# Writing both parts of the first layer's weights to DRAM in the first batch and loading them ready-made in batches 2 to 4

## The chip, the cores and the metric

The kernel runs on one core of a Trainium2 chip. The metric is the device time of one launch in microseconds (us). Five engines have instruction streams of their own: TensorE (PE, matmuls), VectorE (DVE), ScalarE (ACT), GpSimd (POOL) and SyncE (SP, which here issues every DMA). They meet only at semaphores, and each takes its own instructions strictly in order, so an instruction that waits holds up everything behind it on its engine.

## The reference

```
attention:  phi(x) = [exp(p), exp(-p)],  p = x w_phi - max|x w_phi|       (q, k: 4 x 8 x 576 x 64, 128 features)
            out = phi(q) (phi(k)^T v) / (phi(q) sum phi(k) + 1e-6)        -> x: 2304 x 512
layer 1:    h = x w_in (512 x 2048);  g = max(0.01 h, h);  x = g w_out (2048 x 512)
layer 2:    4 experts: x = sum_e p_e * (relu(x w1_e) w2_e)                (512 x 1024, 1024 x 512)
```

All inputs and the output are float32 except w_in and w_out, which arrive as 64-bit floats.

## The kernel before

**Two parts.** Most float32 operands are split into a high part, rounded to the matmul's `fp32r` format, and a low part, the rest. `hilo` (L113) makes them: one copy (ACT for the weights, L117) and one subtraction on DVE (L118). A product is then three matmuls: high by high, high by low, low by high.

**Stages.** The four batches' attention, layer 1 and layer 2 overlap. `attn` (L415) gives each attention step a due time from a table, `moe1_group` (L550) makes the steps of layer 1, and all steps are sorted by due time and recorded (L860). A scheduler then fixes the order on each engine. Layer 1 of batch b is interleaved with the attention of batch b + 1, so the x of a batch (tiles `xh`, `xl`, made by `x_mul`, L367) is due when its layer 1 begins. The last step of the attention chain runs: the denominators `ds` by DMA (L352), a reciprocal on DVE (L359, L360), a store `dr` (L362), a broadcast load `rb` (L364), two multiplications `xr` (L378), then `xh` on ACT and `xl` on DVE. Layer 2 begins at about 640 us.

**Layer 1.** A batch has 16 blocks of 128 hidden columns, F = 0 to 15 in the first batch. `moe1_up` (L494) multiplies x by one w_in tile into the PSUM tile `hp` (24 matmuls of 288 columns, L503), ACT scales it (`hs`, L515), DVE takes the maximum (`g`, L517), and `hilo` makes `gt`. `moe1_down` (L526) multiplies four blocks' `gt` with four w_out tiles into `op` (L535, 24 matmuls for each of four output slices); DVE adds to `acc` (L548). `ORDER` (L26) mixes the four up blocks of a group with the four down slices of the group before. `hp`, `op` and `pq` share three PSUM buffers (`ps2`, L101).

**The weights of layer 1.** Names in the traces: `r` from w_in or w_out is the 64-bit raw tile (two blocks, 1024 KB), `w` the float32 tile (128x512, pool `wrp`), `wt` the tile with both parts (128x1024, pool `wp`), `w_0_f` or `w<-w` the DRAM copy, `wr` a float32 tile loaded back.

- In the first batch, `w64_split` (L449) turns a block of 64-bit numbers into float32 with one ACT instruction (L457) and three on DVE (L458, L461, L464), sends the float32 tile to DRAM (L468) and splits it into `wt`.
- In batches 2 to 4, `w_dma` (L430) loads the float32 tile back into a `wr` tile and `w_split` (L434) splits it again, with one ACT copy and one DVE subtraction for each of 2 x 16 x 3 = 96 tiles.
- `w` and `wr` tiles share the four buffers of `wrp`. A `w` buffer is free when the split has read it and its store to DRAM has landed. `wt` tiles have seven buffers; the first layer-2 weights also use them (L664, L671).

Of the kernel before, what the change touches and what calls it, by code (L numbers as in the profile page):

```python
# [7 lines left out]
F32 = mybir.dt.float32  # L8
F32R = mybir.dt.float32r
# [5 lines left out]
B, H, S, D = 4, 8, 576, 64  # L15
# [51 lines left out]
VHI = ({"g", "w"}, {"k", "q"}, {"k"})  # L67

N_U = 19
N_W = 7  # L70
N_G = 6
N_X = 10

# [6 lines left out]
def body(ctx, tc, kT, qT, vh, w_phi, w_in, w_out, probs, w1, w2, out):  # L80
    nc = tc.nc
# [5 lines left out]
    drw = ec(tc.tile_pool(name="drw", bufs=1, space=bass.MemoryType.DRAM))  # L87

    def opened(stack, name, bufs, **kw):
        return stack.enter_context(  # L90
            tc.tile_pool(name=name, bufs=bufs, reuse_waits="tile", **kw)
        )


    left, left0, right = ExitStack(), ExitStack(), ExitStack()
    up = opened(right, "up", N_U, side="right")
    wp = opened(left0, "wp", N_W)
    vp = opened(left0, "vp", 2)
    wrp = opened(left0, "wrp", 4)
    gp = opened(left0, "gp", N_G)  # L100
    ps2 = opened(left0, "ps2", 3, space=bass.MemoryType.PSUM)  # L101
    ps1 = opened(left0, "ps1", 2, space=bass.MemoryType.PSUM)
# [10 lines left out]
    def hilo(hi, lo, src, name, b):  # L113
        if name in VHI[min(b, 2)]:
            nc.vector.tensor_copy(hi, src)
        else:
            nc.scalar.copy(out=hi, in_=src)  # L117
        nc.vector.tensor_tensor(out=lo, in0=src, in1=hi.bitcast(F32), op=ALU.subtract)  # L118
# [296 lines left out]
    def attn(b, lo, hi):  # L415

        A = []
        for p in range(NP):
            T = TIMES[p if b == 0 else NP]
            for t, (f, h, a) in zip(T, STEPS):  # L420
                i = p if h is None else 2 * p + h
                A.append((p + t, lambda f=f, i=i, a=a: f(b, i, *a)))
        A.sort(key=lambda x: x[0])
        t0, t1 = A[0][0], A[-1][0]
        return [(lo + (hi - lo) * (t - t0) / (t1 - t0), f) for t, f in A]


    raw = {}

    def w_dma(key, src):  # L430
        raw[key] = wrp.tile([128, 512], F32, tag="wr", name="wr")
        nc.sync.dma_start(out=raw[key], in_=src)

    def w_split(key, b, r=None):  # L434
        t = wp.tile([128, 2, 512], F32R, tag="w", name="wt")
        hilo(t[:, 0], t[:, 1], raw.pop(key) if r is None else r, 'w', b)
        return t

    def w64_dma(i, f):

        t = xp.tile([128, 2, 512, 2], U32, tag="x", name="r64")
        nc.sync.dma_start(
            out=t.rearrange("p a c t -> p a (c t)"),
            in_=(w_in, w_out)[i][f : f + 2].bitcast(U32).rearrange("a p c -> p a c"),
        )
        raw[i, f] = t[:, 0]
        raw[i, f + 1] = t[:, 1]

    def w64_split(i, f):  # L449

        r = raw.pop((i, f))
        lo, hi = r[:, :, 0], r[:, :, 1]
        w = wrp.tile([128, 512], F32, tag="wr", name="w32")
        wu = w.bitcast(U32)


        nc.scalar.activation(out=w, in_=hi.bitcast(F32), func=AF.Abs, scale=2.0**-112)  # L457
        nc.vector.tensor_scalar(  # L458
            out=wu, in0=wu, scalar1=3, scalar2=None, op0=ALU.logical_shift_left
        )  # L460
        nc.vector.scalar_tensor_tensor(  # L461
            out=wu, in0=hi, scalar=0x80000000, in1=wu, op0=ALU.bitwise_and, op1=ALU.bitwise_or
        )
        nc.vector.scalar_tensor_tensor(  # L464
            out=wu, in0=lo, scalar=29, in1=wu, op0=ALU.logical_shift_right, op1=ALU.bitwise_or
        )
        d = drw.tile([128, 512], F32, name=f"w32_{i}_{f}")
        nc.sync.dma_start(out=d, in_=w)  # L468
        w32[i, f] = d
        return w_split(None, 1, w)  # L470

    w32 = {}
    wt1 = {}

    def w1_dma(i, F):
        b, f = divmod(F, NF)
        if b == 0:
            if f % 2 == 0:
                w64_dma(i, f)
        elif b < B:  # L480
            w_dma((i, F), w32[i, f])

    def w1_split(i, F):
        b, f = divmod(F, NF)
        if b < B:
            wt1[i, F] = w64_split(i, f) if b == 0 else w_split((i, F), b + 1)

    PASS = ((0, 0), (0, 1), (1, 0))
    accs = {}
# [60 lines left out]
    def moe1_group(G):  # L550


        def up(F, n):
            if n == 0:
                w1_dma(0, F + 2)
                w1_split(0, F + 1)
                w1_dma(1, F)
            elif F:
                w1_split(1, F - 1)
            moe1_up(F, n)  # L560

        def down(d, n):
            if G == B * NF // GF and d == 0 and n == 0:
                w1_split(1, G * GF - 1)
            moe1_down(G - 1, d, n)

        M = []
        for kind, i in ORDER:
            if kind == "u" and G < B * NF // GF:
                M += [lambda i=i, n=n: up(G * GF + i, n) for n in range(2)]  # L570
            elif kind == "d" and G > 0:
                M += [lambda i=i, n=n: down(i, n) for n in range(2)]
        return M
# [88 lines left out]
    def w2_dma(c):  # L662

        pool, tag = (m2["r"], "r") if m2 else (wp, "w")  # L664
        r = pool.tile([128, 4, 256], F32, tag=tag, name="r")
        nc.sync.dma_start(out=r[:, 2:4].rearrange("p a f -> p (a f)"), in_=w1[2 * c])
        nc.sync.dma_start(out=r[:, 0:2].rearrange("p a f -> p (a f)"), in_=w1[2 * c + 1])
        return r
# [170 lines left out]
    def spread(fs, lo, hi):  # L839
        return [(lo + (hi - lo) * i / len(fs), f) for i, f in enumerate(fs)]  # L840

    def first():
        w1_dma(0, 0)
        w1_dma(1, 0)
# [5 lines left out]
    for b in range(B):  # L850
# [3 lines left out]
        if b + 1 < B:  # L854
            a = attn(b + 1, b + LO[b], b + HI[b])
        else:
            early = x2_steps(0)
            a = spread(early[:4], b + 0.1, b + 0.9)
# [10 lines left out]
    r = w2_dma(0)  # L869
# [17 lines left out]
    r = w2_dma(1)  # L887
    r2 = w2_dma_d(0)
    nxt = []
    for k in range(n):  # L890
        j, c = divmod(k, NC2)
# [4 lines left out]
        r = w2_dma((k + 2) % NC2) if k + 2 < n else None  # L896
# [38 lines left out]
```

## Time and profile before

| | |
|---|---|
| median of 3 runs | 1399.87 us (1398.96 to 1400.92) |
| the profiled execution | 1398.86 us, span 1397.1 us |
| PE busy | 1355.4 us (97%) |
| DVE, ACT, POOL busy | 816.9, 658.4, 572.7 us |
| granted TensorE clock, mean | 0.989 |

The span runs from the first instruction to the last; the execution's own time is 1.8 us longer. Overlapping matmuls count as busy PE, so PE time is lost where PE waits for another engine, or where its granted clock is low. PE stalls, their releasers and the chain that ended last are what to read; a busy share of another engine says little by itself.

### The profile page before, as it was taken

What the parts mean: (1) busy time and instruction counts of PE and PEld (TensorE: products, weight loads), DVE (VectorE), ACT (ScalarE), POOL (GpSimd) and SP (SyncE); (2) the same over time, 40 slices, a digit from 0 to 9 for tenths busy, and PEclk for the clock granted to TensorE, in tenths of its full rate; (3) what the DMA queues carried; (4) which work ended last, traced back from release to release, by engine and by line L of the source; (5) the groups of instructions that cost most, each with busy time, mean ns of one, the idle gap of its engine ahead of it and who ended that gap; (6) DMA issues with size and microseconds to landing.
All of it is one profiled execution on the core that took longest, in us unless ns stands there. A gap on an engine that the chain in (4) does not pass through costs nothing.

```text
span 1397.1 us, 21274 instructions
## 1 busy us (share of the span) xinstructions
PE 1355.4 (97%) x8105; PEld 1264.4 (91%) x8105; DVE 816.9 (58%) x1285; ACT 658.4 (47%) x1201; POOL 572.7 (41%) x398
## 2 busy tenths in 40 slices
PE   8769989999999999999999999999999999999998
PEld 6668989999999999998999899999999999999997
DVE  5359879877777566554454544454445544454445
ACT  5547755676566544433344433444344333333331
POOL 3123101111111000015676675667677675656551
PEclk9979999999999999999999999999999999999999
DMA  6348554333332232222211221321212131212111
GB/s 218 95 120 299 199 201 126 124 107 102 113 102 78 78 105 79 69 69 76 76 61 61 76 69 67 112 70 61 76 62 74 61 119 63 76 61 76 61 61 61
DMA packets 78038, 134.94 MB, mean 97 GB/s; under 512 B 11760, under 2 KB 22128, under 8 KB 77936
## 3 DMA queue, kind: packets, MB, share of 16 engines
q1 hardware_dynamic: 77936, 133.58, 29.2%
q8 instruction: 64, 1.05, 0.3%
q14 instruction: 38, 0.31, 0.1%
HBM read 120.30 MB, written 13.18 MB: 96 GB/s over the span
## 4 chain that ended last, share of the span: by engine, by line
PE 86%; DMA 6%; DVE 4%; issue 2%; ACT 1%; POOL 0%; SPq 0%; DVEq 0%; ACTq 0%; POOLq 0%
PE po L758 28%; PE op L535 13%; PE hp L503 12%; PE py L719 11%; PE pv L719 7%; PE px L719 7%; PE kvp L242 4%; PE nm L335 2%; DMA rb<-dr 2%; DMA qraw<-qT 2%; PE pk L204 2%; DMA w<-w 1%; DMA r<-w_in 1%; PE pq L292 1%; DVE w L461 1%
## 5 line engine op out<-in xcount | busy, mean ns | idle before, releaser
L758 PE MATMUL po<-wd,gh 128*128 128x512 f32 x1152 | 387.4, 391 | 0.9 <-POOL wd L711 0.9
L774 DVE SCALAR_TENSOR_TENSOR ob<-po,pe,ob 128x512 f32<-128x512 f32 x270 | 201.6, 749 | 216.5 <-PE po L758 216.5
L758 PEld LDWEIGHTS po<-wd,gh 128*128 128x128 f32 x1152 | 216.3, 188 | 42.5 <-POOL wd L711 1.3
L535 PE MATMUL op<-gt,wt 128*128 128x288 f32 x1536 | 222.7, 299 | 6.7 <-DVE g L517 5.3
L296 POOL PARTITION_ALL_REDUCE mb<-pc x32 | 76.9, 2406 | 370.8 <-ACT pc L294 312.6
L758 PE MATMUL po<-wd,gl 128*128 128x512 f32 x576 | 226.0, 392 | 0.0
L503 PE MATMUL hp<-xh,wt 128*128 128x288 f32 x1024 | 216.1, 298 | 3.3 <-ACT xh L117 3.3
L535 PEld LDWEIGHTS op<-gt,wt 128*128 128x128 f32 x1536 | 210.3, 190 | 8.4 <-DVE g L517 5.8
L503 PEld LDWEIGHTS hp<-xh,wt 128*128 128x128 f32 x1024 | 167.5, 188 | 4.3 <-ACT xh L117 3.6
L503 PE MATMUL hp<-xl,wt 128*128 128x288 f32 x512 | 152.2, 297 | 0.4 <-DVE xl L118 0.4
L711 POOL TENSOR_TENSOR wd<-r,wd 128x1024 fp32r<-128x1024 f32 x48 | 115.1, 2397 | 88.8 <-ACT wd L707 88.8
L719 PE MATMUL py<-xo,wuh 128*128 128x384 f32 x576 | 148.2, 338 | 0.7 <-DVE pz L824 0.7
L679 POOL TENSOR_TENSOR rs<-r 128x256 f32<-128x256 f32 x96 | 71.3, 744 | 188.1 <-DMA r<-w 188.1
L701 POOL TENSOR_TENSOR wul<-rs,wuh 128x1024 fp32r<-128x1024 f32 x48 | 115.5, 2406 | 66.2 <-ACT wuh L696 66.2
L701 POOL TENSOR_TENSOR wul<-r,wuh 128x768 fp32r<-128x768 f32 x48 | 88.9, 1851 | 84.9 <-ACT wuh L696 84.9
L758 PEld LDWEIGHTS po<-wd,gl 128*128 128x128 f32 x576 | 108.1, 188 | 15.3
L719 PEld LDWEIGHTS py<-xo,wuh 128*128 128x128 f32 x576 | 104.9, 188 | 4.6 <-DVE pz L824 1.0
L719 PE MATMUL pv<-xo,wuh 128*128 128x384 f32 x384 | 99.0, 339 | 0.0
L719 PE MATMUL px<-xo,wuh 128*128 128x384 f32 x384 | 98.6, 338 | 0.0
L503 PEld LDWEIGHTS hp<-xl,wt 128*128 128x128 f32 x512 | 96.4, 188 | 1.1 <-DVE xl L118 0.7
L719 PE MATMUL py<-xo,wul 128*128 128x384 f32 x288 | 97.2, 338 | 0.0
L804 ACT COPY py<-px 128x384 f32<-128x384 f32 x48 | 22.2, 463 | 143.6 <-PE px L719 137.5
(114 smaller groups left out, 2349.7 us busy)
## 6 DMA issues: line engine op xcount, KB each, us to landing
r<-w SPq DMA_DIRECT2D x192, 256.0 KB, 2.6
wr<-w SPq DMA_DIRECT2D x96, 256.0 KB, 3.3
qraw<-qT SPq DMA_DIRECT2D x32, 288.0 KB, 7.1
r<-w_out SPq DMA_DIRECT2D x9, 1024.0 KB, 9.0
r<-w_in SPq DMA_DIRECT2D x8, 1024.0 KB
w<-w SPq DMA_DIRECT2D x32, 256.0 KB, 2.2
v<-vh SPq DMA_DIRECT2D x16, 480.0 KB, 3.9
kraw<-kT SPq DMA_DIRECT2D x16, 288.0 KB, 5.1
```

The source lines that it names most:

```text
L204: nc.tensor.matmul(o, lhsT=x[:, cs], rhs=w, start=(i == 0), stop=(i == len(P) - 1))
L242: nc.tensor.matmul(kvp[:, a * 128 : (a + 1) * 128], lhsT=lhs, rhs=v[:, c, h * D : h * D + 128], start=(c == 0), stop=(c == 4),)
L296: nc.gpsimd.partition_all_reduce(mb, pc, 128, bass_isa.ReduceOp.absmax)
L335: nc.tensor.matmul(o, lhsT=a[:, 2 * (h % 2) + j], rhs=x[:, j * HS : (j + 1) * HS], start=(j == 0 and i == 0), stop=(j == 1 and i == len(P) ...
L503: nc.tensor.matmul(hp[:, n, 0:HS], lhsT=wi[:, a, kk * 128 : (kk + 1) * 128], rhs=x[z][:, kk, n * HS : (n + 1) * HS], start=(kk == 0 and i ...
L535: nc.tensor.matmul(op[:, n, 0:HS], lhsT=wt1[1, C * GF + f][:, a, d * 128 : (d + 1) * 128], rhs=gts[C * GF + f][:, z, n * HS : (n + 1) * HS ...
L679: kept(nc.gpsimd.tensor_tensor(out=o, in0=x, in1=y, op=op))
L701: kept(nc.gpsimd.tensor_tensor(out=lo[:, at], in0=(r[:, 1:4], s)[i], in1=hi[:, at].bitcast(F32), op=ALU.subtract))
L711: kept(nc.gpsimd.tensor_tensor(out=d[:, 1], in0=r2, in1=d[:, 0].bitcast(F32), op=ALU.subtract))
L719: kept(nc.tensor.matmul(out, lhsT=ws[w][:, AOPS[a], kk * 128 : (kk + 1) * 128], rhs=xo[z][:, kk], start=first and n == 0, stop=n == 5, ski ...
L758: kept(nc.tensor.matmul(op, lhsT=(gh, gl)[z][:, 2 * f + t, q : q + 128], rhs=d[:, w, f], start=n == 0, stop=n == 5,))
L774: kept(nc.vector.scalar_tensor_tensor(out=o, in0=op, scalar=ps, in1=o, op0=ALU.mult, op1=ALU.add))
```

## The change

In the first batch the store to DRAM now takes the finished `wt` tile with both parts (128x1024, 512 KB) in place of the float32 tile (256 KB), so it is issued after the split. In batches 2 to 4 each tile is loaded from there straight into a `wt` buffer, and the 96 copies and 96 subtractions are gone. `w_dma`, `w_split` and the `wr` tiles are gone too; the load is issued in `w1_split`, and waits for a free `wt` buffer. `wp` has eight buffers for seven, `wrp` two for four.

```diff
-N_W = 7
+N_W = 8
...
-    wrp = opened(left0, "wrp", 4)
+    wrp = opened(left0, "wrp", 2)
...
-    def w_dma(key, src):
-        raw[key] = wrp.tile([128, 512], F32, tag="wr", name="wr")
-        nc.sync.dma_start(out=raw[key], in_=src)
-
-    def w_split(key, b, r=None):
-        t = wp.tile([128, 2, 512], F32R, tag="w", name="wt")
-        hilo(t[:, 0], t[:, 1], raw.pop(key) if r is None else r, 'w', b)
-        return t
...
-        d = drw.tile([128, 512], F32, name=f"w32_{i}_{f}")
-        nc.sync.dma_start(out=d, in_=w)
+        t = wp.tile([128, 2, 512], F32R, tag="w", name="wt")
+        hilo(t[:, 0], t[:, 1], w, 'w', 1)
+        d = drw.tile([128, 1024], F32, name=f"w32_{i}_{f}")
+        nc.sync.dma_start(out=d, in_=t.bitcast(F32).rearrange("p a c -> p (a c)"))
         w32[i, f] = d
-        return w_split(None, 1, w)
+        return t
...
     def w1_dma(i, F):
         b, f = divmod(F, NF)
-        if b == 0:
-            if f % 2 == 0:
-                w64_dma(i, f)
-        elif b < B:
-            w_dma((i, F), w32[i, f])
+        if b == 0 and f % 2 == 0:
+            w64_dma(i, f)
 
     def w1_split(i, F):
         b, f = divmod(F, NF)
-        if b < B:
-            wt1[i, F] = w64_split(i, f) if b == 0 else w_split((i, F), b + 1)
+        if b == 0:
+            wt1[i, F] = w64_split(i, f)
+        elif b < B:
+            t = wp.tile([128, 2, 512], F32R, tag="w", name="wt")
+            nc.sync.dma_start(
+                out=t.bitcast(F32).rearrange("p a c -> p (a c)"), in_=w32[i, f]
+            )
+            wt1[i, F] = t
```

The scheduler makes a new order from this. Lines after the change are numbered lower: L448 is the old L457, L449, L452 and L455 are L458, L461 and L464, L511 and L513 are L515 and L517, L433 is L442; L461 is now the store of a `wt` tile and L479 the load of one.

**Place 1: ACT, late in the first batch, around the conversion of block 15 of w_in (`w32_2199` before, `w32_2197` after).** `hs_1900` belongs to block 11. In brackets stand the semaphores that an instruction waits for; those that begin with DMAHW count landed DMAs. Before:

```order
L275 CAST qr_1875<-qraw_1832 128x576 [waits DMAHW1_49]
L342 COPY nf_1824<-nm_1865 128x288 [waits PE_49]
L342 COPY nf_1747<-nm_1869 128x288 [waits PE_49]
L457 ACTIVATE w32_2199<-r64_1907 128x512 [waits DMAHW4_49,DVE_49]
L515 ACTIVATE hs_1900<-hp_1852 128x576 [waits PE_49]
L117 CAST wt_2045<-w32_2038 128x512
```

After:

```order
L342 COPY nf_1824<-nm_1865 128x288 [waits PE_49]
L342 COPY nf_1747<-nm_1869 128x288 [waits PE_49]
L511 ACTIVATE hs_1900<-hp_1852 128x576 [waits PE_49]
L117 CAST wt_2043<-w32_2038 128x512 [waits DMAHW4_49,DVE_49]
L117 CAST gt_1904<-g_1902 128x576 [waits DVE_49]
L117 CAST wt_2066<-w32_2061 128x512 [waits DMAHW0_49,DVE_49]
L511 ACTIVATE hs_1956<-hp_1921 128x576 [waits PE_49]
L448 ACTIVATE w32_2197<-r64_1907 128x512 [waits DVE_49]
```

The conversion has moved behind `hs_1900` and waits for no DMA any more; the copies into `wt` now wait for one, the store of the tile that had the buffer before.

**Place 2: SP, from the last store of `dr` in the first batch to the load of `rb` that follows it.** Before:

```order
L362 DMA dr<-ds 128x9
L432 DMA wr<-w_0_1_622 128x512
L468 DMA w_1_13_2238<-w_2233 128x512
L166 DMA qraw<-qT 128x576
L442 DMA r_2209<-w_out 128x2x1024
L364 DMA rb<-dr 128x1x576
```

After:

```order
L362 DMA dr<-ds 128x9
L166 DMA qraw<-qT 128x576
L433 DMA r_2207<-w_out 128x2x1024
L461 DMA w_0_15_2205<-wt 128x1024
L364 DMA rb<-dr 128x1x576
```

Before, a load into `wr` and the store of block 13 of w_out's float32 tile stood ahead of `qraw`, the 1024 KB load and `rb`; now `qraw` and the large load go first, and `rb` stands behind the store of block 15 of w_in, which waits for that block's subtraction.

**Place 3: DVE, the conversions of four tiles late in the first batch: 1909 and 2038 (w_in, blocks 13 and 14), 1934 and 2061 (w_out, blocks 11 and 12).** After:

```order
L118 TENSOR_TENSOR wt<-w_1909,wt 128x512
L118 TENSOR_TENSOR wt<-w_1934,wt 128x512
L118 TENSOR_TENSOR gt<-g,gt 128x576
L449 TENSOR_SCALAR w_2038<-w_2038 128x512
L276 TENSOR_TENSOR qr<-qraw,qr 64x576
L452 SCALAR_TENSOR_TENSOR w_2038<-r_1907,w_2038 128x512
L449 TENSOR_SCALAR w_2061<-w_2061 128x512
```

Tile 2038 has the buffer of 1909, and 2061 that of 1934: two and four DVE instructions stand between the subtraction that frees a buffer and the first DVE instruction on the next tile, and in that time ACT must have run L448. Before, with four buffers, the same two tiles' first instructions stood ahead of the subtraction of 1934:

```order
L118 TENSOR_TENSOR wt<-w_1909,wt 128x512
L458 TENSOR_SCALAR w_1934<-w_1934 128x512
L458 TENSOR_SCALAR w_2038<-w_2038 128x512
L461 SCALAR_TENSOR_TENSOR w_1934<-r_1780,w_1934 128x512
L461 SCALAR_TENSOR_TENSOR w_2038<-r_1907,w_2038 128x512
L458 TENSOR_SCALAR w_2061<-w_2061 128x512
```

What has moved is how far the conversions run ahead of each other.

## Rows read from the trace of the kernel before

**Rows 1.** The page: busy us, share of the span, instructions of each engine.

```profile
PE 1355.4 (97%) x8105; PEld 1264.4 (91%) x8105; DVE 816.9 (58%) x1285; ACT 658.4 (47%) x1201; POOL 572.7 (41%) x398
```

**Rows 2.** Busy time by window: length, PE, PEld, DVE, ACT, POOL, clock, DMA share, GB/s.

```profile
250.00:625.00 375.00, 374.82 (x2882) 374.78 (x2883) 258.19 (x392) 211.97 (x406) 32.44 (x17) 1.00 0.31 95
208.00:216.00 8.00, 5.21 (x23) 5.21 (x24) 6.38 (x13) 5.20 (x9) 0.00 (x0) 0.57 0.27 82
```

**Rows 3.** PE's waits in 250 to 625 us: total, times, longest.

```profile
PE pq L292 <- DVE g L517: 0.9, 1, 0.9
```

**Rows 4.** Groups by line in 250 to 625 us: busy us, mean ns, idle before.

```profile
L118 DVE TENSOR_TENSOR wt<-wr,wt 128x512 fp32r<-128x512 f32 x94 | 63.6, 695 | 19.9 <-ACT wt L117 19.8
L117 ACT CAST wt<-wr 128x512 fp32r<-128x512 f32 x92 | 54.1, 617 | 31.8 <-PE op L535 19.4 <-PE hp L503 9.0 <-DMA wr<-w 3.3
```

**Rows 5.** ACT's and DVE's waits in 90 to 255 us: total, times, longest.

```profile
ACT w L457 <- DMA w<-w: 10.7, 3, 7.0
...
DVE w L458 <- ACT w L457: 10.2, 5, 5.7
DVE xr L378 <- DMA rb<-dr: 7.4, 2, 6.6
```

**Rows 6.** The chain that ended last: start us, us, what.

```profile
199.27 9.39 DMA w<-w
...
225.88 11.39 DMA rb<-dr
...
593.32 9.54 PE hp L503 x72
...
612.42 6.36 PE op L535 x48
```

**Rows 7.** Timeline of ACT: start us, us, instruction, idle before and its releaser.

```profile
208.75 0.66 ACT L457 ACTIVATE w<-r 128x512 f32<-128x512 f32 x1 [6.96 <-DMA w<-w]
209.31 0.63 ACT L515 ACTIVATE hs<-hp 128x576 f32<-128x576 f32 x1
...
628.19 0.67 ACT L117 CAST gt<-g 128x576 fp32r<-128x576 f32 x1 [0.82 <-DVE g L517]
```

**Rows 8.** Timeline of PE.

```profile
210.79 7.59 PE L535 MATMUL op<-gt,wt 128*128 128x288 f32 x39 [4.61 <-DVE g L517]
...
243.25 0.38 PE L503 MATMUL hp<-xl,wt 128*128 128x288 f32 x1
```

**Rows 9.** Timeline of SP, DMA issues.

```profile
213.61 0.33 SPq L362 DMA_DIRECT2D dr<-ds  x1
...
224.55 0.32 SPq L468 DMA_DIRECT2D w<-w  x1
...
225.88 0.54 SPq L364 DMA_DIRECT2D rb<-dr  x1
```

**Rows 10.** Timeline of DVE.

```profile
209.44 0.43 DVE L458 TENSOR_SCALAR w<-w 128x512 uint32<-128x512 uint32 x1 [5.67 <-ACT w L457]
...
211.25 0.17 DVE L359 TENSOR_SCALAR ds<-ds 128x9 f32<-128x9 f32 x1
...
226.98 0.68 DVE L118 TENSOR_TENSOR wt<-w,wt 128x512 fp32r<-128x512 f32 x1
...
241.76 0.75 DVE L118 TENSOR_TENSOR xl<-xr,xh 128x576 fp32r<-128x576 f32 x1
```

**Rows 11.** DVE alone by window: length, busy, clock, DMA share, GB/s.

```profile
90.00:250.00 160.00, 143.88 (x241) 0.96 0.53 188
210.00:230.00 20.00, 19.88 (x31) 0.86 0.37 120
```

**Rows 12.** DMA issues, whole run: count, KB each, median us to landing.

```profile
w<-w SPq DMA_DIRECT2D x32, 256.0 KB, 2.2
...
v<-vh SPq DMA_DIRECT2D x16, 480.0 KB, 3.9
```

**Rows 13.** GB/s moved in 40 slices of 90 to 255 us.

```profile
GB/s 82 55 81 172 402 414 413 147 216 170 192 406 248 107 111 113 30 76 393 416 361 168 282 377 139 113 269 156 49 28 126 49 66 338 142 236 77 7 105 292
```

**Rows 14.** Timeline of POOL where layer 2 begins.

```profile
624.43 1.13 POOL L679 TENSOR_TENSOR rs<-r,rs 128x256 f32<-128x256 f32 x1
```

## The prediction

> **What bounds the kernel now.** I read the page first: PE is busy 97% of the span [rows 1], so work taken off other engines counts only where PE waits for it. Then the windows: from 250 to 625 us, which holds layer 1 of batches 2 to 4, PE is busy 374.82 of 375 us at full clock [rows 2], and its only wait there is 0.9 us, for `g`, at the window's start [rows 3]. That stretch is bound by PE's own instructions, and the change takes none of them away. What the change can move is before 250 us, so I took the waits of ACT and DVE from 90 to 255 us, where layer 1 of the first batch runs, and the chain that ended last.
>
> There the store to DRAM shows. ACT's conversion L457 waited three times, 10.7 us in all, longest 7.0, for the landing of a store `w<-w`, because the store keeps one of four `wrp` buffers; DVE waited 10.2 us for L457, longest 5.7 [rows 5]. The chain has a store that took 9.39 us [rows 6], though the median store lands in 2.2 us [rows 12]: this one was issued behind other transfers. At 208.75 us the conversion starts after 6.96 us of idle ACT, with `hs` of a finished block queued behind it until 209.31 [rows 7]; DVE had stood still for 5.67 us [rows 10], and PE stood 4.61 us until `g` gave back a PSUM buffer [rows 8]. The granted clock was 0.57 from 208 to 216 us [rows 2], a mix of the full 2.4 GHz and 1.2 GHz.
>
> **The change, part by part.**
>
> *The 96 copies and 96 subtractions.* 94 subtractions take 63.6 us of DVE and 92 copies 54.1 us of ACT in 250 to 625 us [rows 4]. They lie beside PE, which waits for nothing there. I cost their removal at 0. The cover that hides them is PE's own work; it stays as it is.
>
> *The 96 loads of 512 KB straight into `wt`.* A load now waits on SP for a `wt` buffer, with attention transfers queued behind it. The buffers come free in bursts, when a group's last down slices have used their four w_out tiles. The first tile then needed is the one for the third up block after that: two up blocks later at least, and three take 9.54 us for 72 matmuls, so 6.36 us [rows 6]. A 480 KB load lands in 3.9 us at the median [rows 12]; 512 KB by size in 4.2. The other loads of the burst are needed later still. PE loses 0; the bounds are 0 and, for a load that took as long as the slowest transfer of the chain, 11.39 us [rows 6], some 5 us once.
>
> *The store.* 256 KB more for each of 32 tiles. At the 414 GB/s that a busy slice shows [rows 13], 262144 bytes take 0.63 us; for the 30 tiles after 90 us, 19 us of transfer in 160 us whose DMA share is 0.53 [rows 11], so 0.65. That is hidden unless something waits behind it, which comes below. The Trainium skill's page "DMA: Bandwidth & Descriptors", section "Where 436 GB/s comes from", puts the HBM limit of a core at about 358 GB/s and so speaks against doubling the stores; by it each would cost 0.73 us and the 30 some 22 us, but the slices with 402 to 416 GB/s lie above that limit.
>
> *The wait for the store.* It leaves `wrp`: the conversion now waits only for DVE. It comes back at the copies into `wt`, on the buffer's last store. Those buffers come round after eight tiles, 30 tiles in 160 us or 43 us at the mean pace; against that even 9.39 us plus 0.63 is short. So the wait goes. PE gets back the 4.61 us, and the slow clock behind it: 39 matmuls took 7.59 us [rows 8], and at the pace of 48 in 6.36 [rows 6] they take 5.17, so 2.4 us more. **Together 7.0 us.** The other two waits held PE for next to nothing, so 0.
>
> The granted clock fell around a wait of 4.61 us and rose again while PE worked. The Trainium skill's page "TensorE: Matmul & The Clock Gate", section "Terms", prices throttled time at one minus the granted share; by that the 0.57 over 8 us costs 3.4 us, waiting PE included, and the sum would be 1.0 us larger. I keep the pace of the matmuls.
>
> *What is late next: x of the second batch.* PE took up its first `hp` with the last quarter of x at 243.25 us [rows 8], and that `xl` ended at 242.51 [rows 10]: 0.7 us of slack. If PE comes 7.0 us earlier, x must come 6.3 us earlier too. Its chain: the reciprocal at 211.25 us stood behind DVE's 5.67 us [rows 10], so `dr`, issued at 213.61, can move by 5.7. `rb` was issued at 225.88, behind a store that waited for DVE until 224.55 [rows 9], and took 11.39 us to land, for which DVE waited [rows 5, 6]. Now `rb` stands behind the store of block 15 of w_in, which needs that block's subtraction, until now the one at 226.98 to 227.66 [rows 10]. Moved by 5.7 this is 222.0, so `rb` gains 2.5 us; 0.63 for the larger store leaves 1.9. In its favour, the 1024 KB load no longer goes out half a microsecond ahead of `rb`. If that lets `rb` land in the 3.9 us of a load of 480 KB [rows 12], it gains 7 us more and x is in time. So of the 7.0 us between 0 and 4.4 (7.0 less 0.7 less 1.9) is lost again. I take 3.0: nearer the upper end, because DVE is busy 19.88 of 20 us from 210 to 230 [rows 11] and can hardly bring that subtraction forward.
>
> *Two `w` buffers for four.* ACT must convert the next tile between the subtraction that frees a buffer and DVE's next instruction on it, and the new order leaves two DVE instructions for that at one tile of Place 3 and four at the other. With four buffers the trace does not show this wait, so I bound it: 0, or a whole conversion of 0.66 us [rows 7] for each of 28 tiles, 18.5 us of DVE. DVE gets back the 10.2 us that it waited for L457 [rows 5], 0.36 us a tile. I take a cost of 0 to PE, since two instructions of about 0.7 us hide one of 0.66.
>
> *The start of layer 2.* Its first loads now stand behind two loads of 512 KB, 1.3 us more at 414 GB/s. GpSimd's last sum would end at 626.9 for 625.56 [rows 14], and ACT's copy of it now stands ahead of the last `gt`, which began at 628.19 [rows 7]. With some 1 us for the copy it just fits; 0, at most 1 us.
>
> **The sum.** 7.0 gained less 3.0 is 4.0. The profiled execution took 1398.86 us, 1.0 below the median of the runs. 1398.86 - 4.0 = 1394.9, and with the 1.0 for the median, **1396.0**; kept gains of 2.6 to 7.0 give 1393 to 1397.5.
>
> **The rivals.**
>
> *All of it is kept.* `rb` goes out early and lands fast, x is in time, and the 0.9 us before `pq` [rows 3] goes as well: 1399.87 - 7.9 = 1392. For it speaks that the large load leaves before the store; against it, the full DVE.
>
> *Nothing is left.* x sets the end of the first batch whatever PE does before it: the stall moves from 206 us to 236 us and again costs clock: 1399.5. For it speaks the slack of only 0.7 us.
>
> *Slower: ACT and DVE in lockstep on two buffers.* Each conversion waits for a subtraction and each DVE step for a conversion, with ACT often held by another wait in between. From 90 to 250 us DVE is busy 143.88 of 160 us [rows 11], so it has 16 us of idle time, 10.2 of which the change frees. It decides from 0.36 us a tile on. At 0.66 us, 18.5 less 10.2 is 8.3 us of DVE; if PE feels half of that and has no gain to set against it, 1404. Against it speaks that DVE's order has other work between.
>
> That the change doesn't do what it says is no rival here, as the order has no copy left in batches 2 to 4; that this saves nothing there is in the forecast.
>
> **How the numbers follow.** Forecast 0.34, all kept 0.18, nothing left 0.24, slower 0.24. A measurement here tells 0.2% from no change, 2.8 us: below 1397.1 is faster, above 1402.7 slower. Faster: 0.18, and four fifths of the forecast, 0.27: 0.45. Slower: 0.24 less the part of it under 1402.7, 0.04, so 0.20, plus 0.02 from a late load: 0.22. The same: the rest, 0.33. The likeliest case alone reaches from 1393 to 1397.5. The range of 8 in 10 takes in the case with all kept and the lockstep at its price, with 1 us on either side: 1391 to 1405.
>
> **What would show it.** Right: no wait of the conversion (now L448) for a store; PE's stall near 206 us and the low clock after it gone; from there to some 620 us PE without gaps and the same length; a new PE wait of some 3 us before the second batch's `hp`, released by `xl` or `xh`. Wrong: DVE waiting for L448 at many tiles (lockstep); PE waiting for a load into `wt` after 250 us, which would price the bursts; or copies into `wt` that wait for a store.

## The result, and the profile after

The change made the kernel slower: 1413.62 us (median of 4 runs, 1412.20 to 1414.32) beside 1399.41 us for the kernel before on the same chip; the ratio is 1.0101, 95% interval 1.0089 to 1.0114. The forecast was 1396.0, with a range of 1391 to 1405.

The page after, beside [rows 1], has 96 instructions fewer on DVE and 96 on ACT, 55 and 48.5 us less work there, and nothing gained by it:

```profile
PE 1361.2 (96%) x8105; PEld 1267.5 (90%) x8105; DVE 761.7 (54%) x1189; ACT 609.9 (43%) x1105; POOL 570.4 (40%) x398
```

Busy time by window in the changed kernel, with the columns of [rows 2]:

```profile
250.00:625.00 375.00, 372.17 (x2842) 371.15 (x2842) 200.61 (x300) 167.07 (x320) 31.01 (x14) 0.99 0.47 157
...
90.00:250.00 160.00, 141.15 (x961) 133.21 (x962) 138.86 (x230) 96.89 (x192) 19.71 (x8) 0.96 0.68 239
```

The kernel before from 90 to 250 us (its line for 250 to 625 us is in [rows 2]):

```profile
90.00:250.00 160.00, 148.88 (x1039) 142.54 (x1039) 143.88 (x241) 102.92 (x206) 25.00 (x9) 0.96 0.53 188
```

From 90 to 250 us the DMA share went from 0.53 to 0.68, and PE was busy 141.15 us; in the kernel before it was 148.88. The waits of the changed kernel in 90 to 255 us (total, times, longest), beside [rows 5]:

```profile
ACT wt L117 <- DVE w L455: 15.2, 11, 4.2
ACT w L448 <- DVE wt L118: 13.7, 11, 5.4
...
DVE xr L378 <- DMA rb<-dr: 8.8, 2, 8.0
DVE ds L359 <- DMA ds<-nf: 7.7, 2, 4.7
DVE qr L273 <- DMA qraw<-qT: 5.3, 1, 5.3
```

The wait of the conversion for a store is gone, as forecast. In its place ACT waits 13.7 us for the subtraction that frees one of the two `w` buffers (2.0 us before), and DVE, in order, stands before `ds` (0.3 us before) and `qraw` (0.2). The three longest stalls of PE after 96 us show where part of that lands:

```profile
220.29 2.08 PE L531 MATMUL op<-gt,wt 128*128 128x288 f32 x11 [3.35 <-DVE gt L118]
...
248.71 0.52 PE L499 MATMUL hp<-xh,wt 128*128 128x288 f32 x1 [2.13 <-DMA wt<-w]
...
448.71 1.60 PE L531 MATMUL op<-gt,wt 128*128 128x288 f32 x10 [2.73 <-DVE g L513]
```

The first is the stall of [rows 8] come back 10 us later: the granted clock was 0.84 from 216 to 224 us. What held it was `ds`: in DVE's timeline the `gt` that PE needed stands right behind it.

```profile
219.40 0.17 DVE L359 TENSOR_SCALAR ds<-ds 128x9 f32<-128x9 f32 x1 [3.03 <-DMA ds<-nf]
219.48 0.75 DVE L118 TENSOR_TENSOR gt<-g,gt 128x576 fp32r<-128x576 f32 x1
```

The second is block 0 of the second batch, whose `wt` tile was loaded and came too late. The third stands in the stretch that was called bound by PE alone. Its cause is in SP's and DVE's timelines:

```profile
430.44 1.75 SPq L479 DMA_DIRECT2D wt<-w  x4
434.48 0.51 SPq L352 DMA_DIRECT2D ds<-nf  x1
435.09 0.52 SPq L166 DMA_DIRECT2D qraw<-qT  x1
435.98 0.32 SPq L479 DMA_DIRECT2D wt<-w  x1
439.05 0.48 SPq L352 DMA_DIRECT2D ds<-nf  x1
```

```profile
446.10 0.17 DVE L359 TENSOR_SCALAR ds<-ds 128x9 f32<-128x9 f32 x1 [6.49 <-DMA ds<-nf]
...
447.90 0.76 DVE L513 TENSOR_TENSOR g<-hp,hs 128x576 f32<-128x576 f32 x1
```

A `ds` tile comes by two transfers of 2.2 KB. Four loads of 512 KB go out at once; the first part of `ds`, a `qraw` of 288 KB and a fifth load follow. The second part of `ds` is issued behind them at 439.05; DVE waits 6.49 us for it, with the `g` behind it that gives PE its next PSUM buffer.

How far the kernels have fallen behind is read best from the first matmul of an up block (PE's timeline, us; F counts blocks from the first batch on, so 16 is block 0 of the second):

| F | 1 | 11 | 16 | 19 | 35 | 39 | 63 |
|---|---|---|---|---|---|---|---|
| before | 98.1 | 196.3 | 237.0 | 271.9 | 424.7 | 463.6 | 621.8 |
| change, later by | 2.3 | 7.8 | 11.7 | 12.7 | 11.1 | 15.9 | 15.8 |

Of the 15.8 us, 11.7 were lost by the start of the second batch, and 4.8 with the stall near 446 us; some was given back between. But 7.8 us were gone at F11, before any of the three stalls. From 100 to 210 us PE's waits, for attention results and one `g`, come to 8.3 us; in the kernel before they come to 3.4 us there, ahead of its own stall. The longest of them (PE's waits in 90 to 255 us: total, times, longest):

```profile
PE nm L335 <- DVE ky L216: 2.7, 2, 1.6
...
PE pq L292 <- DVE qr L276: 1.5, 1, 1.5
...
PE hp L499 <- DVE g L513: 1.4, 1, 1.4
```

Which part of the change makes each of these late was not traced.

### The profile page after: what moved, and what is told of

Same layout as the page of the kernel before. It is cut to its first block, busy times and chain, and to the rows that moved or that the text cites. A ratio compares the mean times of both kernels' runs of the same rounds, so it can differ in the third digit from the quotient of the medians.

```text
span 1412.5 us, 20980 instructions
## 1 busy us (share of the span) xinstructions
PE 1361.2 (96%) x8105; PEld 1267.5 (90%) x8105; DVE 761.7 (54%) x1189; ACT 609.9 (43%) x1105; POOL 570.4 (40%) x398
## 4 chain that ended last, share of the span: by engine, by line
PE 82%; DVE 7%; DMA 7%; issue 2%; ACT 1%; SPq 1%; POOL 0%; POOLq 0%; DVEq 0%; ACTq 0%
PE po L754 28%; PE op L531 11%; PE py L715 11%; PE hp L499 10%; PE pv L715 7%; PE px L715 7%; PE kvp L242 3%; PE nm L335 2%; DMA qraw<-qT 2%; DMA ds<-nf 1%; DMA rb<-dr 1%; PE pk L204 1%; DVE wt L118 1%; DVE w L455 1%; DMA wt<-w 1%
## 5 line engine op out<-in xcount | busy, mean ns | idle before, releaser
L296 POOL PARTITION_ALL_REDUCE mb<-pc x32 | 72.9, 2280 | 388.7 <-ACT pc L294 367.5
L499 PE MATMUL hp<-xh,wt 128*128 128x288 f32 x1024 | 219.0, 300 | 8.8 <-ACT xh L117 5.3
L511 ACT ACTIVATE hs<-hp 128x576 f32<-128x576 f32 x64 | 41.7, 652 | 102.3 <-PE hp L499 102.2
## 6 DMA issues: line engine op xcount, KB each, us to landing
r<-w_out SPq DMA_DIRECT2D x9, 1024.0 KB, 11.7
```

The lines of the kernel that those rows point to most:

```text
L296: nc.gpsimd.partition_all_reduce(mb, pc, 128, bass_isa.ReduceOp.absmax)
L499: nc.tensor.matmul(hp[:, n, 0:HS], lhsT=wi[:, a, kk * 128 : (kk + 1) * 128], rhs=x[z][:, kk, n * HS : (n + 1) * HS], start=(kk == 0 and i ...
L511: nc.scalar.mul(out=hs3, in_=hv, mul=0.01)
```

## The experiments

All were measured beside the kernel before; its median was 1398.85 to 1399.64 us. An interval of a ratio is about 0.13% wide on either side, 1.8 us. Theory A: the added bytes. B: two `w` buffers for four. C: the later place of the store, and the order that comes with it. Each edit also makes the scheduler order its instructions anew, so a difference of 2 us between two kernels is not argued from. In x3, x5, x7, x10, x14 and x16 batches 2 to 4 get the high part of the weights alone, and in x6 and x15 the same 256 KB in both places of the tile: these kernels are there for their time alone.

### First round: one thing at a time

**x1**, the kernel before:

```diff
+    wrq = opened(left0, "wrq", 2)
-        w = wrp.tile([128, 512], F32, tag="wr", name="w32")
+        w = wrq.tile([128, 512], F32, tag="wq", name="w32")
```

> The kernel before, with one thing of the change alone: the assembled float32 `w` of the first batch comes from a pool of two buffers of its own instead of the four it shared with the later loads. Stores, loads and splits are those of before. Theory A (the added bytes on SP's queue make small transfers late): no part of A is here, 1399 us, within 4. Theory B (two buffers for four serialise the conversion with the store or the split, so `wt` comes late from the fourth up block on): most of the loss is here already, 1407 to 1415 us, and the fourth up block starts some 4 us later.

1413.18 us, ratio 1.010 (1.0086 to 1.0113). Two buffers alone cost as much as the whole change; but here stores still hold them, and ACT waited 12.7 us for stores, which the change doesn't. So x16 was made later.

**x2**, the changed kernel with `N_W = 7` and `wrp` of 4:

> The changed kernel with the buffers of before: four `w` buffers and seven `wt` for two and eight. The wide stores and loads stay. Theory A: 1410 to 1416 us, with `ds` still taking 6 to 7 us to land once behind a burst of loads. Theory B: back to 1399 to 1403 us. If both hold a part, between.

1412.80 us, 1.0101 (1.0087 to 1.0115). The old buffers give nothing back as long as the traffic is wide.

**x3**, the changed kernel:

```diff
-        d = drw.tile([128, 1024], F32, name=f"w32_{i}_{f}")
-        nc.sync.dma_start(out=d, in_=t.bitcast(F32).rearrange("p a c -> p (a c)"))
+        d = drw.tile([128, 512], F32, name=f"w32_{i}_{f}")
+        nc.sync.dma_start(out=d, in_=t[:, 0].bitcast(F32))
...
-            nc.sync.dma_start(
-                out=t.bitcast(F32).rearrange("p a c -> p (a c)"), in_=w32[i, f]
-            )
+            nc.sync.dma_start(out=t[:, 0].bitcast(F32), in_=w32[i, f])
...
-                    lhsT=wi[:, a, kk * 128 : (kk + 1) * 128],
+                    lhsT=wi[:, a if F < NF else 0, kk * 128 : (kk + 1) * 128],
```

> The changed kernel with the bytes of before: only the first half of each `wt` is stored and only it is loaded, 256 KB each; in batches 2 to 4 the matmuls take the first half in place of the second, so the low part of the weights is left out there, with as many matmuls. Buffers, store after the split, loads straight into `wt` and the missing splits stay as in the change. Theory A: the loss goes, 1397 to 1403 us, no DVE wait of more than 5 us for `ds`, and no PE wait of over 1 us for a load into `wt`. Theory B (buffers) and theory C (the store that now waits for the subtraction, or another order of the attention work): 1409 to 1415 us still.

1408.58 us, 1.0070 (1.0056 to 1.0083). Half the bytes give back 5 us of 14: neither theory alone. (The matmuls of `op` take the first part in the same way.)

**x4**, the changed kernel with `nc.scalar.dma_start` for `ds` (L352):

> The changed kernel, its bytes and buffers untouched; only the small transfers `ds` are issued from ACT's queue instead of SP's, so they no longer stand behind stores and loads on it. Theory A in the form that counts the queue (first in, first out): `ds` lands in 2 to 3 us, DVE no longer waits 4.7 and 6.5 us for it, PE's stalls near 217 and 446 us go with the slow clock behind the second, 1403 to 1408 us. Theory A in the form that counts the DMA engines themselves (full whatever the queue): `ds` still takes 5 to 7 us, 1411 to 1416 us. Theories B and C: no gain, 1411 to 1416 us.

1405.73 us, 1.0044 (1.0032 to 1.0057): 7.9 us come back. Near 440 us DVE waits less than half as long:

```profile
438.83 0.17 DVE L359 TENSOR_SCALAR ds<-ds 128x9 f32<-128x9 f32 x1 [2.68 <-DMA ds<-nf]
```

In the first batch `ds` was still waited for (6.3 us for 7.7), and the stall near 220 us stayed (3.61 us). At F35 this kernel was 6.0 us behind the kernel before (the change 11.1), at F39 8.2 (15.9). So what stands ahead on the queue explains more than half of the third loss, 2.2 us in place of 4.8. Most of the 7.9 us came back ahead of it; how was not traced, and the first stall has more behind it.

### Second round: each half of the change

**x5**, the kernel before: the split first, then a store of 512 KB; the loads read its first 512 columns.

> Half of the change, in the buffers of before: the first batch splits the tile first and stores both parts, 512 KB, as the change does; batches 2 to 4 load 256 KB and split them, as before (what they load is the high part, so the low part of the weights is left out there). If the first batch's share of the loss is the wide store (bytes or position): lost time up to block 15 as in the change, some 5 to 8 us, and none after: 1405 to 1409 us. If the loss is all from the loads of batches 2 to 4: 1398 to 1401 us. If buffers are needed for it: 1398 to 1401 us too.

1403.87 us, 1.0038 (1.0025 to 1.0050). In its profiled execution all the loss stands ahead of the second batch: 9.1 us at block 16, 7.6 at F63.

**x6**, the kernel before: its own first batch; then `wt` filled by `w32[i, f].unsqueeze(1).to_broadcast([128, 2, 512])`.

> The other half, in the buffers of before: the first batch stores 256 KB of float32 before the split, as before; batches 2 to 4 fill `wt` with a load of 512 KB (the 256 KB read into both of its parts, so the parts are not the weights' own) and split nothing. If the wide loads cost what the trace of the change shows, block 16 waits some 2 to 3 us for its load with slow clock behind it, and near 440 us DVE waits some 6 us for `ds`: 1404 to 1409 us. If the whole loss comes from the first batch: 1398 to 1401 us.

1403.49 us, 1.0032 (1.0019 to 1.0045). DVE waited 6.35 us for `ds` at 433.68 us; block 16 came on time.

**x7**, the kernel before: `d` stores `t[:, 0]` after the split.

> The kernel before with one thing moved: the store of the first batch goes out after the split instead of before it, with the bytes of before (256 KB; it is the high part of the tile that is stored, so the low part of the weights is left out in batches 2 to 4). Theory C (the store's place, and the order of the other engines that comes with it): the first batch's share is here, 1404 to 1408 us. Theory A (bytes): 1397 to 1401 us, since SP waits longer but moves no more.

1397.81 us, 0.9989 (0.9980 to 0.9998). Theory C falls: the place of the store costs nothing, and the hold on the `w` buffer is gone. Beside x5 the wider store costs 6.1 us in this code.

**x8**, the kernel before with the edit of x4:

> The kernel before, only `ds` issued from ACT's queue. If what this gave the changed kernel (7.9 us) was that `ds` escapes the wide transfers ahead of it on SP's queue, there is little to escape here: 1397 to 1401 us. If it was mostly another order of the attention work, or a cost that the kernel before has too: 1390 to 1396 us, faster than both.

1399.62 us, 1.0004 (0.9995 to 1.0013). So the 7.9 us of x4 are no gain that this queue gives to any order of the work: they come only with the wide traffic (and are 3.1 with the old buffers, x13 below).

### Third round: the gain by itself, and a test that decides nothing

**x9** and **x11**, the changed kernel and the one before:

```diff
-        nc.vector.tensor_scalar(out=ds, in0=ds, scalar1=1e-6, scalar2=None, op0=ALU.add)
-        nc.vector.reciprocal(ds, ds)
+        nc.gpsimd.tensor_scalar(out=ds, in0=ds, scalar1=1e-6, scalar2=None, op0=ALU.add)
+        nc.gpsimd.tensor_tensor(out=ds, in0=ds, in1=uno, op=ALU.pow)
```

(`uno` holds -1.)

> The changed kernel with its traffic and buffers untouched; the reciprocal of `ds` is taken on GpSimd instead of DVE, so no instruction of DVE waits for the transfer `ds`, however late it lands. If the added bytes reach PE mainly because DVE, in order, stands behind `ds` with a block's `g` and `gt` queued after it: the stalls of 3.5 us near 217 and 2.9 us near 446 go with their slow clock, 1402 to 1407 us. If PE would have waited anyway (for x or the weights that come late): 1410 to 1416 us.

> The kernel before with the reciprocal of `ds` on GpSimd, the control of x9. Its stall near 206 us was put down to the store that keeps a `w` buffer, and there ds is waited for little: 1397 to 1402 us. If `ds` holds DVE there too: 1392 to 1397 us, faster than both.

1456.48 us (1.0413) and 1447.93 us (1.0350): the test cost far more than what it was to measure, and decides nothing. POOL's timeline of x11 shows why:

```profile
48.68 4.30 POOL L296 PARTITION_ALL_REDUCE mb<-pc  x2 [6.09 <-issue]
59.96 0.28 POOL L361 TENSOR_SCALAR ds<-ds 128x9 f32<-128x9 f32 x1 [6.97 <-issue]
60.32 1.85 POOL L362 TENSOR_TENSOR ds<-ds,uno 128x9 f32<-128x9 f32 x1
68.06 2.15 POOL L296 PARTITION_ALL_REDUCE mb<-pc  x1 [5.89 <-issue]
```

Between the all-reduce and the ordinary instructions GpSimd stood 5.9 to 7.0 us in these lines, up to 9.1 further on, waiting for nothing that the profile shows; and it now stood before `ds` itself, with `mb` of the next heads queued behind.

**x10**, x3 with the buffers of before:

> As x3_half_bytes (256 KB stored after the split, 256 KB loaded straight into `wt`, the low part left out in batches 2 to 4), now with the buffers of before, four and seven. x3 still lost 9 us with the bytes of before. If two `w` buffers are what is left there (theory B): 1398 to 1402 us. If it is the order that the missing splits bring, or any schedule but that of before: 1405 to 1410 us.

1396.53 us, 0.9977 (0.9969 to 0.9986): faster than before, with the low part left out. So at half the bytes two `w` buffers (with eight `wt` for seven) cost 12.1 us (x3), and at the old buffers the bytes cost 16.3 (x2).

**x12**, the kernel before with `wrp` of 6:

> The kernel before with six `w` buffers for four, nothing else: the conversion no longer waits for a store. This is the prediction's gain taken alone, without more bytes. By the prediction: the stall of 4.61 us near 206 us goes, 7.0 us less 3.0 given back, 1393 to 1397 us. By what the change showed (the same burst of transfers holds `ds` and DVE behind it at the same place): the stall stays or moves by a few us, 1398 to 1401 us.

1396.71 us, 0.9982 (0.9973 to 0.9991). The gain that was forecast is real, and smaller: 2.5 us. PE's waits from 195 to 255 us are this one line, in place of the 4.61 us of [rows 8]:

```profile
PE op L535 <- DVE gt L118: 1.4, 1, 1.4
```

Of the versions faster than the kernel before, this is the one that leaves nothing out.

### Fourth round: which bytes, and the buffers with no store to hold them

**x14** and **x15**, x10 with one transfer made 512 KB again. In x15 PE's order is that of x10 all through layer 1, but for six matmuls near 234 us, and DVE's up to some 350 us.

> x10 (1396.5 us: buffers of before, 256 KB each way, loads straight into `wt`) with the full store of 512 KB; the loads stay 256 KB and the low part stays left out in batches 2 to 4. From x10 to x2 both transfers doubled and 16 us were lost. If the stores carry most of it: 1404 to 1410 us, by block 16. If the loads do: 1396 to 1400 us. If only both together do it: 1396 to 1401 us here and in x15.

> x10 with the full load of 512 KB (the 256 KB read into both parts of the tile); stores stay 256 KB, matmuls as in x10. The first batch's instructions stand as in x10. If the loads carry most of the 16 us between x10 and x2: 1404 to 1410 us, with a stall behind `ds` near 440 us. If that stall alone is theirs, as in x6: 1400 to 1403 us, all of it after 400 us. If the loads cost nothing without the wide stores: 1396 to 1398 us.

x14: 1407.47 us, 1.0060 (1.0047 to 1.0073), 10.9 more than x10. x15: 1403.56 us, 1.0032 (1.0019 to 1.0044), 7.0 more. DVE's waits of x14 in 90 to 265 us, and after them x10's for `ds`:

```profile
DVE w L449 <- ACT w L448: 8.7, 2, 5.9
DVE xr L378 <- DMA rb<-dr: 7.4, 1, 7.4
DVE ds L359 <- DMA ds<-nf: 4.8, 2, 3.3
```

```profile
DVE ds L359 <- DMA ds<-nf: 2.9, 3, 1.4
```

ACT in x14 stood 17.7 us before `L448` for the 1024 KB loads of raw weights (12.3 in x10), and its late conversions held DVE, 8.7 us for 5.3; PE stood 3.6 us before `op` and 2.6 before the first loaded `wt` (1.1 and 1.5 in x10).

In x15 more than half of the loss is in one spot. DVE's and PE's timelines of x15, then the same instruction of DVE in x10:

```profile
433.43 0.17 DVE L359 TENSOR_SCALAR ds<-ds 128x9 f32<-128x9 f32 x1 [6.38 <-DMA ds<-nf]
```

```profile
436.02 1.58 PE L531 MATMUL op<-gt,wt 128*128 128x288 f32 x10 [2.59 <-DVE g L513]
```

```profile
429.43 0.17 DVE L359 TENSOR_SCALAR ds<-ds 128x9 f32<-128x9 f32 x1 [2.93 <-DMA ds<-nf]
```

In both kernels five loads into `wt` are issued in the 9 us before this `ds`, which goes out 3.1 us after the fifth (at 426.48 and 425.93 us): the same queue in the same order, with twice the bytes ahead, and from issue to use 6.95 us for 3.50. F35 began at 422.7 (x10) and 423.2 us (x15), F39 at 462.0 and 466.2: some 3.6 us lost between them. Some 2 us more went where layer 1 ends, in three waits of PE for `g`, `gt` and `acc`.

**x16**, x7 with the pool of x1:

> x7 (1397.8 us: splits and loads of before, 256 KB of the high part stored after the split, so that no store holds a `w` buffer) with two `w` buffers for four in the first batch. The bytes are those of before. If two buffers cost time by themselves (ACT's conversion waiting for the subtraction of two tiles before, 14 us in the change and in x3): 1405 to 1412 us. If they cost only together with the changed traffic: 1396 to 1400 us.

1406.74 us, 1.0060 (1.0046 to 1.0074), 8.9 more than x7. With the old bytes, the old loads and no store to hold a buffer, two buffers cost time by themselves. Waits of x16 in 90 to 255 us, its lines numbered one higher (L458 is the conversion):

```profile
ACT wt L118 <- DVE w L465: 13.3, 12, 3.0
ACT w L458 <- DVE wt L119: 10.4, 10, 3.8
```

```profile
DVE ds L360 <- DMA ds<-nf: 11.1, 3, 4.0
```

In x7 the first two were 2.4 and 5.9 us, and DVE waited 6.4 for `ds`. How these waits reach PE is not shown. In the profiled execution the granted clock was 0.80 from 110 to 120 us and 0.69 from 120 to 130, after a wait of PE of 1.57 us for `ky` at 114.54 us (0.92 and 0.91 in x7); the change and x3, with two buffers too, have 1.00 in both. So the cost is there, but part of it is a slow clock at a place where the change has none, and 8.9 us is not the price of the buffers in the change.

**x13**, x2 with the edit of x4:

> The changed kernel with the buffers of before and `ds` on ACT's queue: the wide traffic alone, without the wait for a `w` buffer (ACT 13.7 us in the change) and without `ds` behind wide transfers. If these two waits are how the change reaches PE: 1398 to 1404 us. If other late transfers do it (the 1 MB loads of the raw weights, for which ACT waited 16.6 us in x2, or the first loads into `wt`): 1408 to 1413 us.

1409.73 us, 1.0074 (1.0061 to 1.0086): 3.1 us less than x2. The edit did not take the wait for `ds` away in the first batch (DVE 5.8 us in 90 to 265), so what would be left without it stays open. Beside it ACT stood 14.4 us before `L448` for the raw loads, DVE 8.6 us before `rb`, and PE 2.9 us before the first loaded `wt`: `ds` is not the only transfer that comes late. Near 440 us the edit did what it did in x4: 2.2 us were lost between F35 and F39, and 3.9 in x2.

### What they come to

Medians in us, all with the splits of batches 2 to 4 gone:

| stores, loads | four `w`, seven `wt` | two `w`, eight `wt` |
|---|---|---|
| 256, 256 KB | 1396.5 (x10) | 1408.6 (x3) |
| 512, 256 KB | 1407.5 (x14) | |
| 256, 512 KB | 1403.6 (x15) | |
| 512, 512 KB | 1412.8 (x2) | 1413.6 (the change) |

Down the left column the two costs nearly add up, 10.9 and 7.0 for 16.3. Across, the buffers cost 12 us with the narrow traffic and 1 with the wide. That both make the same tiles of the first batch late, and the later of two delays decides, would explain it; that is argued, not shown. Eight `wt` buffers for seven were not tested by themselves.

Is a new order alone a rival? Four kernels have one, but neither a wider transfer nor two buffers: x7, x8, x10 and x12 stand between 2.7 us under the kernel before and level with it. So none of the new orders tried cost anything by itself, though each of the slower kernels has an order of its own that was not tried alone.

The third stall can be tied to the loads in every run but x9 and x11, which put the reciprocal on GpSimd. Between F35 and F39 the kernels with loads of 512 KB lost 3.9 to 4.8 us against the kernel before (the change, x2, x6, x15), those with such loads and `ds` on ACT's queue 2.2 (x4, x13), and those with loads of 256 KB 0.0 to 0.5 (x1, x3, x5, x7, x8, x10, x12, x14, x16).

## Why the prediction was wrong, point by point

- **What bounds it.** From 250 to 625 us PE was called bound by its own work, and the removal of 96 copies and 96 subtractions costed at 0. The 0 held: x10, without them, stands 1.3 us from x7, which has them. But the stretch was only safe as long as nothing in it waited for a longer queue.
- **The loads: "PE loses 0".** This step failed. The prediction asked when the loaded tile itself was needed, and found time enough; that was nearly right (2.1 us at block 16, in the first burst). It didn't ask who is queued behind a burst. It measured 7.0 us (x15), and the part that was traced, some 3.6 us, was paid through `ds`, a transfer of 2.2 KB that DVE meets in order.
- **The store: "hidden unless something waits behind it".** The condition was named, and then only `rb` was looked at, for 0.63 us. This step failed as well: it measured 10.9 us (x14), 6.1 in the old code (x5 beside x7). The mean DMA share of 0.53 [rows 11] had looked like room; but [rows 13] show slices above 400 GB/s beside slices of 7, and an average says nothing of what waits in the full ones. The section of the Trainium skill that was weighed there ("DMA: Bandwidth & Descriptors", "Where 436 GB/s comes from") spoke against doubling the stores, and the direction was right; its price and mine counted transfer time, and neither counted a wait behind it.
- **The wait for the store.** Right in kind: the wait went, and with it alone 2.5 us (x12; x7 1.8) where 7.0 less 3.0 was forecast. In the change itself the stall came back 10 us later.
- **What is late next.** Half right. That another transfer of the same chain would hold the second batch was foreseen, but for `rb` and `xl`, at the batch's end. It was `ds`, at the very place of the old stall: the kernel before issued `ds` at 201.52 us, while DVE stood for the conversion, and at 211.25 us [rows 10] it was there without a wait. The forecast 3 us wait of `hp` for `xl` or `xh` did not appear.
- **Two `w` buffers: "a cost of 0 to PE".** This step failed too. The rival had the right part and looked at DVE: DVE waited 0.5 us for the conversion, far under 0.36 us a tile. It was ACT that waited, 13.7 us. Alone the buffers cost 8.9 us (x16, a slow clock of its own included), above the rival's net 4. In the change they add 0.8 us to the wide traffic (x2).
- **The start of layer 2.** Costed at 0 to 1 us. The change was 15.8 us behind at F63 and 15.4 at the end of the span, so nothing was lost there in it (some 2 us in x15).
- **The range.** Its upper end was the lockstep alone; three costs set at 0 lie on one side, and no case took two of them together. (1394.9 and 1.0 are 1395.9, not 1396.0; nothing hangs on it.)

## What to carry to other kernels

Ask of every transfer that is made larger not only when its own data is needed, but which small transfers are issued behind it on the queue and which engine meets them in order: here 2.2 KB behind five loads held VectorE 6.5 us. A wait that ends at a stall may cover another that ends just before it; look for what else was landing meanwhile before counting the whole stall as gain. A buffer count is priced on every engine that takes part in the round, the one that refills the buffer included: here ScalarE waited 13.7 us, VectorE 0.5.

## What the runs showed of the hardware that was not expected

From issue to use by DVE the `ds` near 440 us took 7.05 us on SP's queue (the change) and 4.83 on ACT's (x4), with five or six wide loads issued shortly before in both; the issue held ACT 0.47 us there, but 1.77 once in the first batch, so another queue is no free way round. The Trainium skill, "DMA: Bandwidth & Descriptors", section "Issuing engines are not separate DMA queues", has another engine's queue save little but the issuing; x8 agrees (no gain), x4 with its 7.9 us does not, though how much of that is its new order was not separated. And GpSimd stood 6 to 9 us at changes between PARTITION_ALL_REDUCE and ordinary instructions (x11); with 16 short reciprocals on it the kernel took 49 us more. The Trainium skill, "GPSIMD Engine Reference", section "Instruction dispatch", states about 6 us, without an instruction in the profile, for the first call to newly loaded code; the gaps of 5.9 to 6.97 us agree in size, but they came at every change in the lines shown, not once.
